# The two heads' values products of a pair, issued chunk by chunk as two column tiles of one PSUM bank

## The chip, the cores and the metric

The kernel runs on one NeuronCore of a Trainium2 chip. Its time is the device time in microseconds of one execution. A core has TensorE (PE, which multiplies matrices and writes PSUM; its weight loads are shown apart as PEld), VectorE (DVE), ScalarE (ACT), GpSimd (POOL), SyncE (SP, which issues most of the DMAs here) and 16 DMA engines. All arithmetic is in float32.

## The reference

Attention with normalised queries and keys, and then a feed-forward block whose activation is a softmax-weighted linear unit. 8 sequences of 448 tokens, 12 heads of 64, so x has 3584 rows of 768; the hidden width is 1024. The weights come as float64.

```python
q_n, k_n = (rmsnorm(q, g_q), rmsnorm(k, g_k))
scores = scale * np.matmul(q_n, k_n.transpose(0, 1, 3, 2))
scores = scores - np.max(scores, axis=-1, keepdims=True)
attn = np.exp(scores)
attn = attn / (np.sum(attn, axis=-1, keepdims=True) + 1e-09)
attn_out = np.matmul(attn, v)                       # the values product
x = attn_out.transpose(0, 2, 1, 3).reshape(B * S, H * D)
h = x @ w_in
e = np.exp(h - h.max(-1)); sm = e / (e.sum(-1) + 1e-09)
solu = h * sm
out = ((solu - mean) / np.sqrt(var + 1e-06) * g_ln) @ w_out
```

## The kernel before, in words

Attention goes by pairs of heads: `n` counts 48 pairs, six to a sequence (`NP = 6`). The 448 tokens of a sequence are taken as four chunks of 112 (`NJ = 4`, `SP = 112`). For a pair, `load` fetches q, k and v; `norm` squares (ACT), sums (DVE), takes the power -1/2 (POOL) and scales q and k (`qkn`, DVE and POOL); `qk_transpose` transposes both heads at once on PE into `pt` and copies them out with the gain (`qkT`, DVE). Since the heads' 64 columns lie side by side, head 0 stands in partitions 0 to 63 of `qkT` and head 1 in 64 to 127.

`scores(n, j)` multiplies chunk j of the queries with all keys. The two heads use different halves of the array's rows (64x128 tiles at rows 0 and 64) and different PSUM banks of one tile `s`. DVE takes the maximum `nmax`, ACT the exponential into `E` with its sum. `normalise` divides on POOL, one instruction per head. `e_transpose(n, h, half)` transposes `E` of a head on PE, two chunks of keys at a time, through `pe`, and ACT and DVE copy it to `ET`. `values(n, h)` multiplies v with `ET`: four matmuls, one per chunk of keys, accumulate 64 rows of `o`. Head 0 writes partitions 0 to 63 of the one PSUM tile `o`, head 1 partitions 64 to 127: 128x64 tiles of the array at columns 0 and 64. After head 1, DVE copies `o` to `xT`, the transposed x.

The feed-forward block takes 128 tokens at a time: `ff_in` (`h`), `ff_solu`, `ff_transpose` (`pu`) and `ff_out` (`po`). Each float32 matmul that is no transpose stands in the profile as two weight loads and two matmul records; a transpose stands as one of each. So the 384 values matmuls are 768 records of `o`, and a head's four matmuls are "x8".

The order in which the program is written comes from `pair`: between the four `scores` of pair n stand the transposes of `E` and the values of pair n - 1, head 0's values after `scores(n, 1)`, head 1's after `scores(n, 3)`, and then `qk_transpose(n + 1)`. The pieces of the feed-forward of the sequence before are spread over pairs 2 to 6 of each sequence; the first pair of a sequence gets none (below: an unfilled pair). In sequence 0 there is no feed-forward; instead the weights are converted from float64, largely on DVE. At the very end stand the last pair's transposes and values and the feed-forward of the last sequence. The framework then schedules each engine's instructions from this order, so that what stands in an engine's queue differs somewhat from what is written; each engine runs its queue as it stands. Tile pools give the buffers: PSUM has two of `s` or `h` and four of tag `t`, which `pt`, `pe`, `pu`, `po` and `o` share; `ET` has two.

Of the kernel before, what the change touches and what calls it, by code (L numbers as in the profile page):

```python
# [9 lines left out]
FP32 = mybir.dt.float32  # L10
# [8 lines left out]
def kernel(  # L19
# [12 lines left out]
    nc = tc.nc  # L32
    B, H, S, D = q.shape
    DM, DFF = moe_w_in.shape
    P = 128
    NJ = 4              # token chunks of one sequence; chunk j holds the tokens NJ * p + j
    SP = S // NJ
    NP = H // 2         # head pairs: two heads fill the 128 partitions of a transposed operand
    KD = DM // P
    KF = DFF // P  # L40
    HO = DM // 2
# [17 lines left out]
    def setup():  # L59
        nc.gpsimd.memset(mhalf, -0.5)  # L60
        make_identity(nc, ident)
        nc.scalar.dma_start(grow[0:KF, :], moe_g_ln.rearrange("(c p) -> c p", p=P))
        for i, g in enumerate((g_q, g_k)):
            for h in range(2):
                nc.scalar.dma_start(grow[KF + i : KF + i + 1, h * D : (h + 1) * D], g.rearrange("(o d) -> o d", o=1))
        pg = ps_t.tile([P, KF + 2], FP32, tag="t", name="pg")
        nc.tensor.transpose(pg, grow, ident[0 : KF + 2, 0 : KF + 2])
        nc.vector.tensor_copy(gcol, pg)
        # the scores' 1 / sqrt(D) goes with the gain of q
        nc.vector.tensor_scalar(gcol[:, KF : KF + 1], gcol[:, KF : KF + 1], float(D) ** -0.5, None, OP.mult)  # L70

    # The weights come as the bits of float64: word 0 of an element holds the low 32 bits of the
    # mantissa, word 1 the sign, 11 bits of exponent and the high 20 bits of the mantissa.
    # value = M * E, M = 1 + high / 2^20 + low / 2^52 rounded to float32 and E = +-2^(exponent - 1023);
    # E is 0 below the range of float32, and infinite above it.

    def w_steps():
        # the parts to convert, in the order in which they are used
        for c in range(KD):
            for half in range(2):  # L80
                yield moe_w_in, w_in, c, slice(half * 512, half * 512 + 512)
        for c in range(KF):
            for half in range(2):
                yield moe_w_out, w_out, c, slice(half * HO, half * HO + HO)
# [11 lines left out]
    def convert_w(step, raw):  # L96
        _, dst, c, cols = step
        n = cols.stop - cols.start
        lo, hi = raw[:, :, 0], raw[:, :, 1]
        tmp = work.tile([P, 2, n], U32, tag="uT", name="tmp")  # L100
        e, m = tmp[:, 0], tmp[:, 1].bitcast(FP32)
        nc.vector.tensor_scalar(tmp[:, 1], hi, 0xFFFFF, None, OP.bitwise_and)
        nc.scalar.activation(m, tmp[:, 1], AF.Copy, scale=2.0 ** -20, bias=1.0)
        nc.vector.scalar_tensor_tensor(m, lo, 2.0 ** -52, m, OP.mult, OP.add)
        nc.vector.tensor_scalar(e, hi, 20, 0x7FF, OP.logical_shift_right, OP.bitwise_and)
        ei = e.bitcast(I32)
        nc.vector.tensor_scalar(ei, ei, 896.0, 0.0, OP.subtract, OP.max)
        nc.vector.tensor_scalar(ei, ei, 255.0, 2.0 ** 23, OP.min, OP.mult)
        nc.vector.scalar_tensor_tensor(e, hi, 0x80000000, e, OP.bitwise_and, OP.bitwise_or)
        if dst is w_in:  # L110
            nc.gpsimd.tensor_tensor(dst[:, c, cols], m, e.bitcast(FP32), OP.mult)
        else:
            # the gain of the layer norm goes into the rows of w_out
            nc.vector.scalar_tensor_tensor(
                dst[:, c, cols], m, gcol[:, c : c + 1], e.bitcast(FP32), OP.mult, OP.mult
            )

    st = {}
    xTs = {}

# [1 line left out]

    def load(n):
        b, hp = divmod(n, NP)
# [74 lines left out]
    def e_transpose(n, h, half):  # L199
        d = st[n]  # L200
        if half == 0:
            d["ET", h] = work.tile([SP, NJ, S], FP32, tag="ET", name="ET")
        for kc in (2 * half, 2 * half + 1):
            pt = ps_t.tile([SP, S], FP32, tag="t", name="pe")
            for j in range(NJ):
                nc.tensor.transpose(  # L206
                    pt[:, j * SP : (j + 1) * SP], d["E"][:, h, j, kc * SP : (kc + 1) * SP], ident[0:SP, 0:SP]
                )
            (nc.vector.tensor_copy if kc % 2 else nc.scalar.copy)(d["ET", h][:, kc], pt)  # L209

    def values(n, h):
        b, hp = divmod(n, NP)
        d = st[n]
        if b // 2 not in xTs:
            xTs[b // 2] = work.tile([P, KD, 2 * S], FP32, tag="xT", name="xT")
        if h == 0:
            d["o"] = ps_t.tile([P, S], FP32, tag="t", name="o")
        for kc in range(NJ):
            nc.tensor.matmul(  # L219
                d["o"][h * D : (h + 1) * D, :], d["v"][:, h, kc * D : (kc + 1) * D], d["ET", h][:, kc],  # L220
                start=(kc == 0), stop=(kc == NJ - 1),
            )
        if h == 1:
            # back to the order of the tokens
            c0 = (b % 2) * S
            nc.vector.tensor_copy(  # L226
                xTs[b // 2][:, hp, c0 : c0 + S].rearrange("d (p j) -> d j p", j=NJ),
                d["o"].rearrange("d (j p) -> d j p", j=NJ),
            )
            del st[n]  # L230

# [1 line left out]

    mt = {}

# [8 lines left out]
            )  # L244

    def ff_solu(m, t):
        # with u = h * exp(h - max) and s = sum + 1e-9: solu = u / s, so that
        # (solu - mean) / sqrt(var + 1e-6) = (u - mean_u) / sqrt(var_u + 1e-6 * s * s)
        d = mt[m, t]
        nmax = small.tile([P, 1], FP32, tag="hmax", name="hmax")  # L250
        nc.vector.tensor_reduce(nmax, d["h"], AX, OP.max, negate=True)  # L251
        u = d["u"] = work.tile([P, DFF], FP32, tag="u", name="u")
        s = small.tile([P, 1], FP32, tag="hsum", name="hsum")
        nc.scalar.activation(u, d["h"], AF.Exp, bias=nmax, accum_out=s)
        nc.vector.tensor_tensor(u, d["h"], u, OP.mult)
        bs = small.tile([P, 2, 6], FP32, tag="bs", name="bs")
        mv = small.tile([P, 2], FP32, tag="mv", name="mv")
        for half in range(2):
            nc.vector.bn_stats(out=bs[:, half], in_=u[:, half * 512 : half * 512 + 512])
        nc.vector.bn_aggr(out=mv, in_=bs)  # L260
        e = small.tile([P, 1], FP32, tag="he", name="he")
        nc.vector.tensor_scalar(s, s, 1e-9, None, OP.add)
        nc.vector.tensor_scalar(e, s, s, 1e-6, OP.mult, OP.mult)
        nc.vector.tensor_tensor(e, e, mv[:, 1:2], OP.add)  # L264
        nc.gpsimd.tensor_tensor(e, e, mhalf, OP.pow)  # L265
        nc.vector.tensor_scalar(u, u, mv[:, 0:1], e, OP.subtract, OP.mult)
# [23 lines left out]
            del mt[m, t]  # L290

    def feed_forward(b):
        # the tiles of 128 tokens that are whole once sequence b is done
        m, n0 = b // 2, S // P
        tiles = range(0, n0) if b % 2 == 0 else range(n0, 2 * S // P)

        def first(t):
            return [lambda: ff_in(m, t, 0), lambda: (ff_in(m, t, 1), ff_solu(m, t))]

        def second(t):  # L300
            return [lambda: ff_transpose(m, t), lambda: ff_out(m, t, 0), lambda: ff_out(m, t, 1)]

        prev = None
        for t in tiles:
            yield from first(t)
            if prev is not None:
                yield from second(prev)
            prev = t
        yield from second(prev)

    def pair(n):
        # scores of pair n; the values of the pair before it come between them
        pieces = []
        for j in range(NJ):
            pieces.append(lambda j=j: scores(n, j))
            if n:
                h, half = divmod(j, 2)
                pieces.append(lambda h=h, half=half: e_transpose(n - 1, h, half))
                if half:
                    pieces.append(lambda h=h: values(n - 1, h))  # L320
            if j == 1 and n + 3 < B * NP:
                pieces.append(lambda: load(n + 3))
            if j == 1 and n + 1 < B * NP:
# [13 lines left out]
    raw = load_w(wsteps[0])  # L337
    for b in range(B):
        fill = list(feed_forward(b - 1)) if b else []
        # the last pair of a sequence gets its values within the next sequence's first pair  # L340
        flat = [p for i in range(NP) for p in pair(b * NP + i)]
        lead = len(pair(b * NP))
        done = 0
# [13 lines left out]
    for h in range(2):  # L357
        for half in range(2):
            e_transpose(B * NP - 1, h, half)
        values(B * NP - 1, h)  # L360
    for p in feed_forward(B - 1):
        p()

# [29 lines left out]
```

## Time and profile before

| | us |
|---|---|
| time, median of 3 runs | 1561.86 (1561.26 to 1563.79) |
| span of the profiled execution, first to last instruction | 1558.0 |
| the part of the median outside that span | 3.9 |
| PE busy | 1401.2 (90%) |
| DVE, POOL, ACT busy | 783.5, 536.8, 484.3 |
| the scores of sequences 0, 1 and 2 begin in the trace at | 14.9, 191.8, 377.3 |
| the last values product ends at | 1466.9 |

The page has no time of its own for the profiled execution beside the span; the span and the 3.9 us together are taken as its time. The trace thus has three stages: sequence 0 with the conversion of the weights (0 to 192), sequences 1 to 7 with feed-forward work between (192 to 1463), and the last feed-forward alone (to 1558). In rows of instructions "x" is a count; "mean ns" is the length of one record, which for matmuls overlaps with its neighbours, so that the distance from start to start is what an instruction takes of PE. In brackets stands the idle time of the engine before the row and what ended it.

### The profile page before, as it was taken

The numbers are of one execution on the slowest core, as the hardware profiler recorded it, in microseconds if no ns is written. First come the engines' busy times: TensorE is split into PE (matmuls) and PEld (weight loads), VectorE is DVE, ScalarE is ACT, GpSimd is POOL, SyncE is SP. The second block draws the span as 40 slices with busy tenths as digits, with TensorE's granted clock in tenths as the row PEclk, the third lists the DMA queues.
The fourth block names the chain that finished last, engine by engine and source line by source line (L and its number), as shares of the span: only waits on it lengthen the run. The fifth ranks groups of instructions, "written<-read, shape, count | busy, mean of one in ns | idle before, by whom it ended". The sixth has DMA issues, their size and how long they took to land.

```text
span 1558.0 us, 14064 instructions
## 1 busy us (share of the span) xinstructions
PE 1401.2 (90%) x5249; PEld 658.7 (42%) x5249; DVE 783.5 (50%) x1234; ACT 484.3 (31%) x1177; POOL 536.8 (34%) x239
## 2 busy tenths in 40 slices
PE   4676578999899998999899998899899998999998
PEld 2232233444344443444344453344444454444454
DVE  7988874444445444543354434635453344534231
ACT  4333342324223332332333234234322233323111
POOL 5543373333432324334323243343423243231100
PEclk8677779999999999999999999999999999999999
DMA  4322210011010011001000110010100001000000
GB/s 136 111 86 79 85 42 18 28 36 38 19 42 31 18 38 36 18 28 46 29 18 28 33 51 18 24 40 29 46 18 28 29 28 34 6 16 11 11 11 31
DMA packets 42716, 57.53 MB, mean 37 GB/s; under 512 B 3216, under 2 KB 35480, under 8 KB 42648
## 3 DMA queue, kind: packets, MB, share of 16 engines
q1 hardware_dynamic: 38592, 45.62, 9.7%
q10 hardware_dynamic: 4056, 11.02, 1.8%
q8 instruction: 41, 0.67, 0.2%
q14 instruction: 27, 0.22, 0.0%
HBM read 45.62 MB, written 11.01 MB: 36 GB/s over the span
## 4 chain that ended last, share of the span: by engine, by line
PE 65%; DVE 18%; POOL 6%; ACT 5%; DMA 4%; issue 2%; SPq 0%; ACTq 0%; POOLq 0%; DVEq 0%
PE o L219 18%; PE po L285 17%; PE h L242 14%; PE s L180 7%; PE pe L206 7%; POOL E L195 4%; DMA qk<-in_k_dram 3%; DVE nmax L184 3%; PE pt L165 2%; ACT E L186 2%; DVE xT L226 2%; DVE rs L138 2%; DVE qkT L170 2%; POOL rs L144 1%; DVE qkn L152 1%
## 5 line engine op out<-in xcount | busy, mean ns | idle before, releaser
L195 POOL TENSOR_TENSOR E<-E,sum 112x1792 f32<-112x1792 f32 x96 | 305.5, 3201 | 274.0 <-DVE sum L193 261.0
L219 PE MATMUL o<-ET,v 112*64 112x448 f32 x768 | 351.0, 579 | 23.7 <-DVE ET L209 20.4
L242 PE MATMUL h<-w_in,xT 128*128 128x512 f32 x672 | 307.7, 605 | 5.4 <-ACT E L186 5.4
L285 PE MATMUL po<-w_out,uT 128*128 128x384 f32 x896 | 302.2, 490 | 2.1 <-DVE ET L209 1.1
L186 ACT ACTIVATE E<-s,nmax 112x448 f32<-112x448 f32 x384 | 240.2, 632 | 198.0 <-DVE nmax L184 194.8
L184 DVE TENSOR_REDUCE nmax<-s 112x2 f32<-112x896 f32 x192 | 207.1, 1082 | 153.3 <-PE s L180 153.3
L180 PE MATMUL s<-qkT 64*112 64x448 f32 x768 | 214.0, 620 | 47.7 <-DVE qkT L170 36.8
L206 PE MATMUL pe<-ident,E 112*112 112x112 f32 x1536 | 193.2, 273 | 51.2 <-POOL E L195 46.8
L206 PEld LDWEIGHTS pe<-ident,E 112*112 112x112 f32 x1536 | 155.9, 138 | 165.6 <-issue 81.8
L144 POOL TENSOR_TENSOR rs<-rs,mhalf 112x16 f32<-112x16 f32 x48 | 141.9, 2958 | 233.5 <-DVE rs L143 223.8
L285 PEld LDWEIGHTS po<-w_out,uT 128*128 128x128 f32 x896 | 166.0, 190 | 125.3 <-issue 13.8
L242 PEld LDWEIGHTS h<-w_in,xT 128*128 128x128 f32 x672 | 123.8, 192 | 160.5 <-issue 153.2
L219 PEld LDWEIGHTS o<-ET,v 112*64 112x64 f32 x768 | 91.7, 141 | 193.7 <-issue 106.0
L209 ACT COPY ET<-pe 112x448 f32<-112x448 f32 x192 | 101.1, 531 | 192.5 <-PE pe L206 191.4
L209 DVE COPY ET<-pe 112x448 f32<-112x448 f32 x192 | 117.8, 616 | 71.8 <-PE pe L206 70.7
L265 POOL TENSOR_TENSOR he<-he,mhalf 128x1 f32<-128x1 f32 x28 | 15.3, 548 | 319.3 <-DVE he L264 319.3
L180 PEld LDWEIGHTS s<-qkT 64*112 64x112 f32 x768 | 59.6, 182 | 146.2 <-issue 59.0
L251 DVE TENSOR_REDUCE hmax<-h 128x1 f32<-128x1024 f32 x28 | 34.3, 1225 | 168.9 <-PE h L242 168.6
L286 ACT COPY y<-po 128x384 f32<-128x384 f32 x56 | 26.7, 477 | 262.6 <-PE po L285 262.6
L136 ACT ACTIVATE sq<-qk 112x1024 f32<-112x1024 f32 x48 | 50.9, 1060 | 181.5 <-DMA qk<-in_k_dram 150.3
L138 DVE TENSOR_REDUCE rs<-sq 112x16 f32<-112x1024 f32 x48 | 58.4, 1216 | 96.5 <-ACT sq L136 96.5
L152 POOL TENSOR_TENSOR qkn<-qk,rs 112x512 f32<-112x512 f32 x48 | 56.6, 1179 | 137.5 <-PE pt L165 99.9
(43 smaller groups left out, 756.3 us busy)
## 6 DMA issues: line engine op xcount, KB each, us to landing
qk<-in_q_dram SPq DMA_DIRECT2D x48, 224.0 KB, 2.8
qk<-in_k_dram SPq DMA_DIRECT2D x48, 224.0 KB, 3.1
v<-in_v_dram SPq DMA_DIRECT2D x48, 224.0 KB, 2.6
out_dram<-y ACTq DMA_DIRECT2D x28, 384.0 KB, 2.3
raw<-in_moe_w_in_dram SPq DMA_DIRECT2D x12, 512.0 KB, 3.5
raw<-in_moe_w_out_dram SPq DMA_DIRECT2D x16, 384.0 KB, 3.0
grow<-in_g_q_dram ACTq DMA_DIRECT2D x2, 0.2 KB
grow<-in_g_k_dram ACTq DMA_DIRECT2D x2, 0.2 KB
```

What stands on the lines that cost most here:

```text
L138: nc.vector.tensor_reduce(rs.rearrange("p s h j -> p (s h j)"), sq.rearrange("p s h (j d) -> p (s h j) d", d=D), AX, OP.add,)
L144: nc.gpsimd.tensor_tensor(rs.rearrange("p s h j -> p (s h j)"), rs.rearrange("p s h j -> p (s h j)"), mhalf[0:SP].to_broadcast([SP, 4 * NJ ...
L152: eng.tensor_tensor(d["qkn"][:, s].rearrange("p j h d -> p h j d"), d["qk"][:, s].rearrange("p h (j d) -> p h j d", d=D), rs[:, s].rearran ...
L180: nc.tensor.matmul(s[:, h, 0:S], d["qkT"][hh, 0, j * SP : (j + 1) * SP], d["qkT"][hh, 1, :], start=True, stop=True)
L184: nc.vector.tensor_reduce(nmax, s[:, :, 0:S], AX, OP.max, negate=True)
L186: nc.scalar.activation(d["E"][:, h, j], s[:, h, 0:S], AF.Exp, bias=nmax[:, h : h + 1], accum_out=d["sum"][:, h, j : j + 1])
L195: nc.gpsimd.tensor_tensor(d["E"][:, h], d["E"][:, h], d["sum"][:, h].rearrange("p j -> p j ()").to_broadcast([SP, NJ, S]), OP.mult)
L206: nc.tensor.transpose(pt[:, j * SP : (j + 1) * SP], d["E"][:, h, j, kc * SP : (kc + 1) * SP], ident[0:SP, 0:SP])
L209: (nc.vector.tensor_copy if kc % 2 else nc.scalar.copy)(d["ET", h][:, kc], pt)
L219: nc.tensor.matmul(d["o"][h * D : (h + 1) * D, :], d["v"][:, h, kc * D : (kc + 1) * D], d["ET", h][:, kc], start=(kc == 0), stop=(kc == NJ ...
L242: nc.tensor.matmul(d["h"][:, hs], xTs[m][:, c, t * P : (t + 1) * P], w_in[:, c, hs], start=(c == 0), stop=(c == KD - 1))
L285: nc.tensor.matmul(po, d["uT"][:, c], w_out[:, c, hs], start=(c == 0), stop=(c == KF - 1))
```

## The change

`values` no longer takes a head. Called once per pair, at the place of head 1's values before, it goes through the four chunks of keys and issues for each chunk head 0's matmul and then head 1's. The `o` tile lives from there to its copy instead of from head 0's values on. `ET` has three buffers instead of two.

```diff
@@ e_transpose
-            d["ET", h] = work.tile([SP, NJ, S], FP32, tag="ET", name="ET")
+            d["ET", h] = work.tile([SP, NJ, S], FP32, tag="ET", name="ET", bufs=3)
@@ values
-    def values(n, h):
+    def values(n):
...
-        if h == 0:
-            d["o"] = ps_t.tile([P, S], FP32, tag="t", name="o")
+        o = ps_t.tile([P, S], FP32, tag="t", name="o")
         for kc in range(NJ):
-            nc.tensor.matmul(
-                d["o"][h * D : (h + 1) * D, :], d["v"][:, h, kc * D : (kc + 1) * D], d["ET", h][:, kc],
-                start=(kc == 0), stop=(kc == NJ - 1),
-            )
-        if h == 1:
...
+            for h in range(2):
+                nc.tensor.matmul(
+                    o[h * D : (h + 1) * D, :], d["v"][:, h, kc * D : (kc + 1) * D], d["ET", h][:, kc],
+                    start=(kc == 0), stop=(kc == NJ - 1),
+                )
...
@@ pair
-                if half:
-                    pieces.append(lambda h=h: values(n - 1, h))
+                if j == NJ - 1:
+                    pieces.append(lambda: values(n - 1))
@@ the last pair
     for h in range(2):
         for half in range(2):
             e_transpose(B * NP - 1, h, half)
-        values(B * NP - 1, h)
+    values(B * NP - 1)
```

The queue of PE in an unfilled pair (the first of sequence 5), before. Counts here are matmuls of the program, of which `s`, `o`, `h` and `po` have two records each in the profile:

```order
L180 MATMUL s<-qkT 112x448 x2
L206 MATMUL pe<-ident,E 112x112 x8
L180 MATMUL s<-qkT 112x448 x2
L206 MATMUL pe<-ident,E 112x112 x8
L219 MATMUL o<-ET,v 64x448 x4
L180 MATMUL s<-qkT 112x448 x2
L206 MATMUL pe<-ident,E 112x112 x8
L180 MATMUL s<-qkT 112x448 x2
L206 MATMUL pe<-ident,E 112x112 x8
L219 MATMUL o<-ET,v 64x448 x2
L165 MATMUL pt<-ident,qkn 128x112 x2
L219 MATMUL o<-ET,v 64x448
```

Such a pair after the change (the values stand on line 221 now):

```order
L180 MATMUL s<-qkT 112x448 x2
L206 MATMUL pe<-ident,E 112x112 x8
L180 MATMUL s<-qkT 112x448 x2
L206 MATMUL pe<-ident,E 112x112 x8
L180 MATMUL s<-qkT 112x448 x2
L206 MATMUL pe<-ident,E 112x112 x8
L180 MATMUL s<-qkT 112x448 x2
L206 MATMUL pe<-ident,E 112x112 x8
L221 MATMUL o<-ET,v 64x448 x8
L165 MATMUL pt<-ident,qkn 128x112 x8
L206 MATMUL pe<-ident,E 112x112 x12
```

Head 0's four matmuls have moved down past two scores and two transposes, and head 1's, which were split by transposes of q and k, stand together with them.

In the program of before no two neighbouring values matmuls belong to different heads. In the changed one, counted over PE's whole queue, 318 neighbours do. Taken two by two from the front of each run, they make 180 couples of one matmul of each head, out of 192 that are possible; after the fifth pair of heads 165 out of 172. In the first five pairs of heads, transposes of q and k and scores stand between, and three couples are left of four; here the first values of the program, on PE:

```order
L221 MATMUL o<-ET,v 64x448
L180 MATMUL s<-qkT 112x448 x2
L221 MATMUL o<-ET,v 64x448 x2
L165 MATMUL pt<-ident,qkn 128x112 x4
L221 MATMUL o<-ET,v 64x448 x4
L165 MATMUL pt<-ident,qkn 128x112 x4
L221 MATMUL o<-ET,v 64x448
```

The values matmuls stand in 183 runs before and in 66 after. Places in PE's queue at which the shape of the tile changes (128x128, 64x128 for scores, 128x64 for values) are 674 before and 477 after; past the fifth pair's values, 599 and 412.

On DVE the end of the unfilled pair reads so before:

```order
L170 TENSOR_SCALAR qkT<-pt,gcol 128x448
L226 COPY xT<-o 128x4x112
L170 TENSOR_SCALAR qkT<-pt,gcol 128x448
L192 TENSOR_SCALAR sum<-sum 112x8
L152 TENSOR_TENSOR qkn<-qk,rs 112x2x4x64
```

and so after:

```order
L192 TENSOR_SCALAR sum<-sum 112x8
L193 RECIPROCAL sum<-sum 112x8
L227 COPY xT<-o 128x4x112
L170 TENSOR_SCALAR qkT<-pt,gcol 128x448 x2
L209 COPY ET<-pe 112x448
L152 TENSOR_TENSOR qkn<-qk,rs 112x2x4x64
```

The copy of `o` now stands ahead of both copies of `qkT`, and the sums and their reciprocal, on which POOL's division waits, ahead of all three.

More of the change, by code (lines that the diff above doesn't have):

```diff
@@ L215, in values @@
             xTs[b // 2] = work.tile([P, KD, 2 * S], FP32, tag="xT", name="xT")
-        if h == 0:
-            d["o"] = ps_t.tile([P, S], FP32, tag="t", name="o")
+        o = ps_t.tile([P, S], FP32, tag="t", name="o")
         for kc in range(NJ):
-            nc.tensor.matmul(
-                d["o"][h * D : (h + 1) * D, :], d["v"][:, h, kc * D : (kc + 1) * D], d["ET", h][:, kc],
-                start=(kc == 0), stop=(kc == NJ - 1),
-            )
-        if h == 1:
[L225 to L230, printed above, removed]
+            for h in range(2):
[3 more added lines that the diff above has]
+                )
+        c0 = (b % 2) * S
+        nc.vector.tensor_copy(
+            xTs[b // 2][:, hp, c0 : c0 + S].rearrange("d (p j) -> d j p", j=NJ),
+            o.rearrange("d (j p) -> d j p", j=NJ),
+        )
+        del st[n]
     mt = {}
```

## The prediction

> **What bounds the kernel now.** I read the page first: busy times, the slices of the span, and the chain that ended last.
>
> ```profile
> span 1558.0 us, 14064 instructions
> PE 1401.2 (90%) x5249; PEld 658.7 (42%) x5249; DVE 783.5 (50%) x1234; ACT 484.3 (31%) x1177; POOL 536.8 (34%) x239
> PE   4676578999899998999899998899899998999998
> ...
> DVE  7988874444445444543354434635453344534231
> PE 65%; DVE 18%; POOL 6%; ACT 5%; DMA 4%; issue 2%; SPq 0%; ACTq 0%; POOLq 0%; DVEq 0%
> ```
>
> PE is at nine tenths from the fifth of the slices on; DVE is the fuller engine only at the start, and the chain has 65% in PE. The stages, in time windows (busy us of PE, PEld, DVE, ACT, POOL; then the granted clock), and of the first one what the records of `o` alone take:
>
> ```profile
> 0.00:192.00 192.00, 117.42 (x395) 50.10 (x397) 163.52 (x272) 65.33 (x152) 86.46 (x43) 0.75 0.33 101
> 192.00:1463.00 1271.00, 1194.10 (x4594) 562.23 (x4595) 596.45 (x922) 408.00 (x1005) 448.14 (x192) 0.98 0.09 29
> 1463.00:1558.00 95.00, 89.71 (x264) 46.36 (x261) 23.56 (x42) 10.99 (x20) 2.16 (x4) 1.00 0.04 17
> 0.00:192.00 192.00, 46.50 (x80) 10.72 (x80) 4.73 (x5) 0.75 0.33 101
> 377.00:1292.00 915.00, 861.23 (x3316) 407.70 (x3316) 423.23 (x660) 292.89 (x721) 317.96 (x138) 0.99 0.10 31
> ```
>
> So 192 us are mostly DVE's (163.5 busy), 1271 are PE's (94% busy, DVE under half), and 95 are feed-forward alone, which the change does not touch. In five full sequences (last row, 30 pairs of heads) PE is idle for 915 - 861.2 = 53.8 us, 1.8 us per pair. What one PE instruction costs I take from groups by shape (busy us, mean ns) and from the timeline:
>
> ```profile
> L219 PE MATMUL o<-ET,v 112*64 112x448 f32 x768 | 351.0, 579 | 23.7 <-DVE ET L209 20.4 <-ACT ET L209 3.1
> L180 PE MATMUL s<-qkT 64*112 64x448 f32 x768 | 214.0, 620 | 47.7 <-DVE qkT L170 36.8 <-ACT E L186 8.5 <-DVE hsum L262 2.3
> 823.34 3.22 PE L219 MATMUL o<-ET,v 112*64 112x448 f32 x8
> 824.52 0.14 PEld L219 LDWEIGHTS o<-ET,v 112*64 112x64 f32 x1 [0.24 <-issue]
> 824.89 0.14 PEld L219 LDWEIGHTS o<-ET,v 112*64 112x64 f32 x1 [0.24 <-issue]
> 824.52 0.54 PE L219 MATMUL o<-ET,v 112*64 112x448 f32 x1
> 814.46 0.63 PE L180 MATMUL s<-qkT 64*112 64x448 f32 x2
> 814.46 1.01 PE L180 MATMUL s<-qkT 64*112 64x448 f32 x4
> ```
>
> Of `o`, one head's eight records take 3.22 us. The last is 0.54 long, so seven steps take 2.68, 0.383 each; the weight loads step by 0.37 to 0.38. I take 0.376 us of PE per record: they follow each other, none overlaps more than its tail. The scores show the contrast. Same number of records, same 448 columns, but 214.0 us busy against 351.0: two records, one of each head, are both under way within 0.63 us, the length of one, and all four end after 1.01 = one step of 0.38 and one length. Matmuls on two parts of the array do run at once here, in float32, and though each comes as two records.
>
> **The change, part by part.** *Column tiles side by side.* Before, head 0's and head 1's values never stand next to each other; after, 165 couples do past the fifth pair of heads. If a couple runs at once, as the scores' couples do, each saves one matmul, two records: 165 x 2 x 0.376 = 124.1 us of PE. The scores show it for two parts of the rows; here both heads use the same 112 partitions and differ in columns, so PE must read two streams from the same partitions. Nothing in the trace shows two moving streams so. The nearest row is a weight load under a running matmul, which reads the same partitions twice at once: the load at 824.52 begins with the matmul of 824.52, and its successor still follows 0.37 later. Ends: 0 saved (no overlap) and 124.1; I take 124.1, because the scores' row is the nearest.
>
> The Trainium skill, "TensorE: Matmul & The Clock Gate", Part 3 (row/col tiling), has a measured gain of 2.38 for three column tiles, which is 1.26 slots for three; if two needed 1.26 slots as well, an estimate by that page would keep 0.74 of the gain, 92 us instead of 124, and the sum would end 32 us higher.
>
> *Changes of the tile's shape.* The price is in a pair of windows where values follow the feed-forward, beside a run of the latter:
>
> ```profile
> 822.92 0.49 PE L285 MATMUL po<-w_out,uT 128*128 128x384 f32 x1
> 823.34 0.59 PE L219 MATMUL o<-ET,v 112*64 112x448 f32 x1
> 818.07 5.34 PE L285 MATMUL po<-w_out,uT 128*128 128x384 f32 x16
> ```
>
> Sixteen `po` records take 5.34 with a last one of 0.49, so 0.323 from start to start; from the last `po` to the first `o` it is 0.42, 0.09 to 0.10 more. I take 0.093. Past the fifth pair the queue has 599 - 412 = 187 fewer such changes: 17.4 us. Ends: 0, where PE waits there for something else anyway, and 18.
>
> *Sequence 0.* DVE sets most of it, and the clock is 0.75. Its 80 records of `o` occupy 46.5 us; half of that, 23, is the most that could go, nothing the least. What waited there:
>
> ```profile
> DVE qkn L152 <- POOL rs L144: 11.9, 6, 3.0
> ...
> DVE xT L226 <- PE o L219: 5.5, 4, 2.6
> ```
>
> DVE waited for the values for 5.5 us only. I take 4.
>
> *What becomes late next.* In the other 43 pairs PE loses about 3.3 us of work each (141.5 / 43), and its waits can grow, since other engines' work was covered by it. The unfilled pair shows the covers:
>
> ```profile
> 930.80:947.60 16.80, 15.29 (x73) 6.69 (x72) 9.76 (x15) 8.60 (x22) 3.93 (x2) 1.00 0.08 28
> 980.70:1015.40 34.70, 29.91 (x111) 13.21 (x110) 19.38 (x27) 9.90 (x24) 12.99 (x7) 0.90 0.11 34
> 946.13 0.94 DVE L226 COPY xT<-o 128x448 f32<-128x448 f32 x1 [0.59 <-PE o L219]
> 947.48 0.16 DVE L192 TENSOR_SCALAR sum<-sum 112x8 f32<-112x8 f32 x1
> 947.62 0.63 PE L180 MATMUL s<-qkT 64*112 64x448 f32 x2 [1.53 <-DVE qkT L170]
> 948.52 6.30 POOL L195 TENSOR_TENSOR E<-E,sum 112x1792 f32<-112x1792 f32 x2 [2.20 <-DVE sum L193]
> 951.75 1.75 PE L206 MATMUL pe<-ident,E 112*112 112x112 f32 x16 [2.36 <-POOL E L195]
> ```
>
> DVE and ACT have 9.8 and 8.6 us of work in it, so at 16.8 - 3.3 = 13.5 us they still fit; the fuller pair has 19.4 us of DVE in 34.7. No engine becomes the bound by its amount of work. The waits at its end are 1.53 (the copies of `qkT`, behind the copy of `o` on DVE) and 2.36 (POOL's division, which began only once DVE, behind those copies, had done the sums). In the new DVE queue the sums stand ahead of these copies, so POOL starts while the eight values matmuls run. `qkT` comes as late as before: copy of `o` and two `qkT` copies after the last values. I take 1 us off for each of the 7 unfilled pairs (between 2.4 off and 1 more). In the 36 filled pairs I add 0.4 us each, a little over a fifth of the 1.8 they wait on average; the ends are 0 (the feed-forward covers) and 3.3 (everything saved is waited). The nearest row for it is the list of what PE waits for past 192 us, which is short and spread:
>
> ```profile
> PE pe L206 <- POOL E L195: 24.2, 14, 3.1
> PE s L180 <- DVE qkT L170: 15.4, 8, 4.7
> PE o L219 <- DVE ET L209: 13.2, 7, 3.1
> ...
> PE pu L275 <- ACT ET L209: 5.9, 7, 1.5
> ```
>
> The third `ET` buffer lets the next pair's first head be transposed while both old `ET` are still read; it costs no instruction. That `o` holds a shared PSUM buffer for a few us instead of half a pair can only ease waits like the last row's; I count nothing. The loads of q, k and v move little on SP, and their covers stay: nothing above waits for a DMA in the middle stage.
>
> *Sum.* 1558.0 - 124.1 - 17.4 - 4 - 7 + 14 = 1419.5 us; with the 3.9 us by which the median of the runs is above the span, 1423.
>
> **The rivals.** *No overlap.* Column tiles may run one after the other, and the change then does not do what it says. For it: no row shows two streams from the same partitions. Against: the scores. Only the 17.4 us of shape changes are left: 1562 - 17 = 1545, still faster.
>
> *Slower.* Without overlap, alternating columns could also expose the weight load at each step from one head to the other: 318 steps x 0.14 us (the length of a load in the row at 824.52) = 45 us, less the 17.4: 1562 + 27 = 1589. It decides once a step costs more than 17.4 / 318 = 55 ns. For it: in no row does a load into other columns run under a matmul. Against: loads into the very same columns do, at 824.89 in the middle of a run.
>
> The Trainium skill, same page and part, says that a weight load overlaps a running matmul only when the row group differs, and here both heads use the same rows; by that rule this rival would come. The trace already disagrees for the single head: loads and matmuls of `o` share all rows, and the step is 0.38 and not 0.38 + 0.14.
>
> *Waits take half back.* The overlap comes, but filled pairs wait for `ET`, `E` and `qkT` half of what they saved: 36 x 1.65 = 59 instead of 14, so 1468. For it: `values` now needs both heads' last copies, with the copies made just ahead. Against: the same wait stood before head 1, and DVE is busy 423 of 915 us.
>
> *One step more per pair.* If matmuls start strictly in order, a couple's second record and the next head's first overlap only staggered: nine steps in place of eight, 43 x 0.376 = 16 us, 1439. This is within the forecast.
>
> **How the numbers follow.** Overlap with waits about as now: 0.72 (own range 1380 to 1460: from 23 instead of 4 us saved in sequence 0, 17 off in unfilled pairs and 0 added in filled ones, to the staggered start with some 20 us of waits more). Waits take half or more: 0.13, up to 1500. No overlap: 0.08. Slower: 0.05; 0.02 for what I did not think of. The range for 8 in 10 takes the first two, less the far ends of the first, which would need all three terms at their best at once: 1390 to 1500. About 0.2% (3 us) is what a measurement of this kernel can tell from no change. Faster by more: 0.72 + 0.13 + 0.07 = 0.92; within: 0.02; slower: 0.06.
>
> **What would show it.** Right: `o` busy near 190 us instead of 351 with a mean still near 540 to 580 ns; a run of sixteen `o` records of about 3.2 us, two under way at a time; the first sequence still near 190 us; an unfilled pair of 13 to 14 us. The shape changes: `pt` following `o` seldom. Wrong: sixteen records in 6.2 us (no overlap), weight loads of `o` with PE idle beside them (slower), or PE's waits for `ET` and `E` of over 100 us in the middle stage (half taken back).

## The result, and the profile after

The changed kernel takes 1441.9 us (median of 4 runs, 1438.2 to 1448.0) against 1562.1 before: a ratio of 0.923, 95% interval 0.921 to 0.926. The forecast was 1423 with a range of 1390 to 1500. The profiled execution took 1442.7 us, its span 1440.9.

Of the page after, the same lines as before, and then two rows of its timeline:

```profile
span 1440.9 us, 14104 instructions
PE 1246.6 (87%) x5249; PEld 630.5 (44%) x5249; DVE 803.3 (56%) x1234; ACT 482.0 (33%) x1177; POOL 548.6 (38%) x239
PE   3466558899899998899899998899899998999998
...
PE 44%; DVE 23%; POOL 12%; DMA 8%; issue 6%; ACT 6%; SPq 1%; ACTq 0%; POOLq 0%; DVEq 0%
L221 PE MATMUL o<-ET,v 112*64 112x448 f32 x768 | 173.1, 558 | 16.2 <-DVE ET L209 15.8
875.77 3.23 PE L221 MATMUL o<-ET,v 112*64 112x448 f32 x16
876.20 0.92 PE L221 MATMUL o<-ET,v 112*64 112x448 f32 x4
```

The same number of values records is busy for 173.1 us in place of 351.0, and each is as long as before (558 ns on average against 579). The last two rows are of one pair of heads: sixteen records in 3.23 us, as long as one head's eight took; in a window 0.1 us wide, four records are in progress, two couples that are 0.38 us apart. PE's share of the chain falls from 65% to 44%, DVE's, POOL's and DMA's rise.

The three stages in time windows (busy PE, PEld, DVE, ACT, POOL; clock):

```profile
0.00:190.30 190.30, 100.64 (x393) 46.10 (x394) 164.16 (x271) 65.36 (x152) 89.91 (x43) 0.72 0.34 102
190.30:1348.90 1158.60, 1059.27 (x4601) 538.68 (x4601) 615.79 (x923) 405.64 (x1005) 456.47 (x192) 0.97 0.10 32
1348.90:1440.90 92.00, 86.70 (x256) 45.75 (x256) 23.38 (x41) 11.00 (x20) 2.17 (x4) 1.00 0.05 18
```

Sequence 0 lasts 190.3 us in place of 191.8 while PE is busy 17 us less in it: it is DVE's, with 164 us busy as before. All but 1.5 us of the gain lies in the seven sequences that follow. (The last window begins here where the values products end; the one of the kernel before began 4 us ahead of that point, so 95 and 92 us are not to be compared.)

To split those into work and waits I took, for each two matmul records that follow each other, the distance of their starts less the step of the first one's kind (0.376 us for `o` and `s`, 0.429 for `h`, 0.3225 for `po`, 0.0957 for `pe` and `pt`, 0.109 for `pu`, 0.093 more where the tile's shape changes; a partner that starts within 0.07 us counts as it is). From the first score of sequence 1 to the end, work falls from 1209.9 to 1068.9 us, by 141.0, and waits rise from 151.4 to 176.8, by 25.4. 141.0 - 25.4 + 1.5 is the 117.1 us by which the span is shorter.

Not all that this split calls a wait is idle time of PE. From the first score of sequence 1 to the end (before, then after, in windows):

```profile
191.80:1558.00 1366.20, 1283.96 (x4856) 608.75 (x4856) 620.21 (x963) 418.99 (x1025) 450.30 (x196) 0.98 0.09 28
190.30:1440.90 1250.60, 1145.97 (x4856) 584.44 (x4856) 639.17 (x964) 416.64 (x1025) 458.64 (x196) 0.97 0.10 31
```

PE is idle for 82.2 us before and 104.6 after, 22.4 more. The rest of the waits, 69 us before and 72 after, are steps that took longer than their kind's while PE was busy; the granted clock was 0.98 before and 0.97 after. So the growth is idle time but for some 3 us.

What PE waits for past sequence 0, after (waited for, us, times, longest), in place of the list that the prediction quotes:

```profile
PE s L180 <- ACT E L186: 27.7, 17, 2.9
PE h L243 <- ACT E L186: 19.6, 13, 2.7
PE pe L206 <- POOL E L195: 12.7, 9, 2.8
PE s L180 <- DVE qkT L170: 11.8, 5, 4.0
```

The first two are new in that size: in the trace before, `s` waited 6.2 us for ACT's exponential there and `h` 5.4. Scores and `h` share two PSUM buffers, and such a buffer comes free when the exponentials have read it. An unfilled pair of 13 to 14 us, one of the signs of being right, did not come: those of sequences 2 to 7 take 15.8 to 19.0. The waits for POOL's division and for `qkT` became shorter (24.2 and 15.4 before).

### The profile page after: what moved, and what is told of

Read it like the earlier page. It is cut to its first block, busy times and chain, and to the rows that moved or that the text cites. A ratio compares the mean times of both kernels' runs of the same rounds, so it can differ in the third digit from the quotient of the medians.

```text
span 1440.9 us, 14104 instructions
## 1 busy us (share of the span) xinstructions
PE 1246.6 (87%) x5249; PEld 630.5 (44%) x5249; DVE 803.3 (56%) x1234; ACT 482.0 (33%) x1177; POOL 548.6 (38%) x239
## 4 chain that ended last, share of the span: by engine, by line
PE 44%; DVE 23%; POOL 12%; DMA 8%; issue 6%; ACT 6%; SPq 1%; ACTq 0%; POOLq 0%; DVEq 0%
PE po L286 15%; PE h L243 14%; POOL E L195 8%; DMA qk<-in_k_dram 7%; PE o L221 6%; PE s L180 5%; DVE nmax L184 5%; PE pe L206 4%; ACT E L186 3%; DVE rs L138 2%; DVE qkn L152 2%; POOL rs L144 2%; DVE qkT L170 2%; POOL qkn L152 2%; ACT sq L136 2%
## 5 line engine op out<-in xcount | busy, mean ns | idle before, releaser
L195 POOL TENSOR_TENSOR E<-E,sum 112x1792 f32<-112x1792 f32 x96 | 309.7, 3247 | 234.6 <-DVE sum L193 233.3
L243 PE MATMUL h<-w_in,xT 128*128 128x512 f32 x672 | 317.3, 622 | 19.6 <-ACT E L186 19.6
L286 PE MATMUL po<-w_out,uT 128*128 128x384 f32 x896 | 306.8, 495 | 14.0 <-ACT ET L209 8.6
L184 DVE TENSOR_REDUCE nmax<-s 112x2 f32<-112x896 f32 x192 | 207.5, 1083 | 140.4 <-PE s L180 140.2
L206 PE MATMUL pe<-ident,E 112*112 112x112 f32 x1536 | 200.8, 277 | 43.2 <-POOL E L195 40.8
L206 PEld LDWEIGHTS pe<-ident,E 112*112 112x112 f32 x1536 | 161.0, 141 | 163.8 <-issue 88.6
L243 PEld LDWEIGHTS h<-w_in,xT 128*128 128x128 f32 x672 | 128.1, 198 | 177.3 <-issue 154.3
L221 PE MATMUL o<-ET,v 112*64 112x448 f32 x768 | 173.1, 558 | 16.2 <-DVE ET L209 15.8
L266 POOL TENSOR_TENSOR he<-he,mhalf 128x1 f32<-128x1 f32 x28 | 15.4, 550 | 299.8 <-DVE he L265 299.8
L227 DVE COPY xT<-o 128x448 f32<-128x448 f32 x48 | 46.5, 968 | 98.5 <-PE o L221 98.2
L221 PEld LDWEIGHTS o<-ET,v 112*64 112x64 f32 x768 | 53.6, 138 | 98.6 <-issue 73.2
```

Source lines behind the costliest of these rows:

```text
L184: nc.vector.tensor_reduce(nmax, s[:, :, 0:S], AX, OP.max, negate=True)
L195: nc.gpsimd.tensor_tensor(d["E"][:, h], d["E"][:, h], d["sum"][:, h].rearrange("p j -> p j ()").to_broadcast([SP, NJ, S]), OP.mult)
L206: nc.tensor.transpose(pt[:, j * SP : (j + 1) * SP], d["E"][:, h, j, kc * SP : (kc + 1) * SP], ident[0:SP, 0:SP])
L221: nc.tensor.matmul(o[h * D : (h + 1) * D, :], d["v"][:, h, kc * D : (kc + 1) * D], d["ET", h][:, kc], start=(kc == 0), stop=(kc == NJ - 1),)
L243: nc.tensor.matmul(d["h"][:, hs], xTs[m][:, c, t * P : (t + 1) * P], w_in[:, c, hs], start=(c == 0), stop=(c == KD - 1))
L286: nc.tensor.matmul(po, d["uT"][:, c], w_out[:, c, hs], start=(c == 0), stop=(c == KF - 1))
```

## The experiments

**Is it overlap, and does it need the heads side by side?** Three kernels keep the change's place, buffers and pieces, and alter only how the two heads stand within a values product.

Head 0 first, then head 1:

```diff
-        for kc in range(NJ):
-            for h in range(2):
+        for h in range(2):
+            for kc in range(NJ):
```

> The changed kernel, but within the values product head 0's four matmuls are issued first and then head 1's four; place, tile, buffers and everything else stay. Theory A (the gain is overlap, and it needs matmuls of different columns next to each other in the queue): only the one joint per pair of heads can overlap, so nearly all of the 124 us comes back; 1441 + 7/8 x 135 = about 1555 us, a run of sixteen records of o takes about 5.8 us. Theory B (PE starts any queued matmul whose columns are free, however the heads are ordered within the run): about 1441 us, a run of 3.2 us. Theory C (the gain is the regrouping, fewer changes of the tile's shape and the later place, not overlap): also about 1441 us, but with runs of o near 6 us.

In blocks of two chunks, so that the heads stand 0 0 1 1 0 0 1 1:

```diff
-        for kc in range(NJ):
-            for h in range(2):
+        for k2, h, i in [(k2, h, i) for k2 in range(2) for h in range(2) for i in range(2)]:
+            kc = 2 * k2 + i
+            if True:
```

> The changed kernel, with the heads alternating in blocks of two chunks (two matmuls of head 0, two of head 1, and again). Theory A with starts strictly in the queue's order: a run of sixteen records needs 13 steps of 0.376 us in place of 8, so 48 x 5 x 0.376 = 90 us come back, about 1531 us. Theory A with a look-ahead of two matmuls, or Theory B: 8 steps, about 1441 us. Theory C: about 1441 us.

Alternating as in the change, but both heads on the same columns:

```diff
-                    o[h * D : (h + 1) * D, :], d["v"]...
-                    start=(kc == 0), stop=(kc == NJ - 1),
+                    o[0:D, :], d["v"]...
+                    start=(kc == 0 and h == 0), stop=(kc == NJ - 1 and h == 1),
...
+        nc.scalar.copy(xTs[b // 2][D:P, ...], o[0:D]...)
```

> The changed kernel with both heads' matmuls on the same columns: order and place as in the change, but head 1 writes partitions 0 to 63 too, accumulated onto head 0 (so the two heads' values are summed, which the reference does not ask), and the sum is copied to both halves of xT, the upper half by ACT. The queue stays as in the change and nothing can overlap. Theories A and B: 180 couples x 2 records x 0.376 = 135 us come back, 1576 us, a run of o near 6.2 us. Theory C: 1441 us, up to 1450 for the second copy.

Measured: 1482.5 us for head after head, 1445.7 in twos, 1534.8 on the same columns, against 1441.9 for the change. A run of sixteen records in each (in this order):

```profile
561.37 4.78 PE L221 MATMUL o<-ET,v 112*64 112x448 f32 x16
549.56 3.28 PE L222 MATMUL o<-ET,v 112*64 112x448 f32 x16
518.01 6.23 PE L221 MATMUL o<-ET,v 112*64 112x448 f32 x16
```

The same column gives 6.23 us, sixteen steps of 0.376 and a tail (the 0.2 us by which the last record is longer than its step): with nearly the same queue nothing overlaps, and the time is 93 us over the change, not the 135 expected. (The same columns are also the same rows of PSUM; these runs do not part the two.) So the gain is overlap of columns, and Theory C falls; without the overlap 1534.8 is left, still 27 to 29 us under the kernel before (its ratio is 0.982, 0.979 to 0.984). Neither A nor B fits head after head: 4.78 us are twelve steps, not sixteen and not eight. Its windows near the start, in the middle and near the end show where the overlap lies:

```profile
561.80 0.91 PE L221 MATMUL o<-ET,v 112*64 112x448 f32 x2
562.92 0.97 PE L221 MATMUL o<-ET,v 112*64 112x448 f32 x4
565.24 0.92 PE L221 MATMUL o<-ET,v 112*64 112x448 f32 x2
```

Two records in progress are one stream and its predecessor's tail; four are two streams. The couples stand in the middle alone, from the fifth step to the eighth: head 1's first four records start beside head 0's last four, ahead of records that stand before them in the queue. That gave a new theory: a record may start beside the oldest waiting one if at most three records stand between them. It fits 0 0 1 1 too, where exactly three do.

**The look-ahead, tried with another order.** 0 0 0 1 1 1 0 1:

```diff
-        for kc in range(NJ):
-            for h in range(2):
+        for h, kc in [(0, 0), (0, 1), (0, 2), (1, 0), (1, 1), (1, 2), (0, 3), (1, 3)]:
+            if True:
```

> The changed kernel with the order 0 0 0 1 1 1 0 1 of the heads in a values product. Theory from the two earlier orders (PE can start a record beside the oldest unfinished one if at most three other unstarted records stand between them): steps are r1, r2, r3 with r7, r4 with r8, r5 with r9, r6 with r10, r11 with r13, r12 with r14, r15, r16: ten steps, a run of 10 x 0.376 + 0.2 = 3.97 us, about 20 us over the change: 1460 us. Rival (only whole blocks of two matmuls pair up): twelve steps or more, a run of 4.7 us or more, 1480 us. Rival (any order overlaps fully within eight matmuls unless one head comes first entirely): 3.2 us, 1442 us.

```profile
552.31 4.03 PE L221 MATMUL o<-ET,v 112*64 112x448 f32 x16
```

4.03 us are ten steps and the tail, as the new theory had it; its couples start after two single steps, and the last two records are single. The time is 1451.7 us, 10 over the change and not 20. The split shows where the rest of the longer runs went: past sequence 0, work is 66 us more than in the change for head after head, 120 on the same columns and 41 here, but waits are 21, 28 and 33 us less. The trace does not name the head of a record; what belongs to which is read from the count of steps.

**The third ET buffer.**

```diff
-            d["ET", h] = work.tile([SP, NJ, S], FP32, tag="ET", name="ET", bufs=3)
+            d["ET", h] = work.tile([SP, NJ, S], FP32, tag="ET", name="ET")
```

> The changed kernel with two ET buffers in place of three; the order of matmuls on PE stays. Theory: the third buffer matters little, since a pair's values end before the next pair's first copies into ET are due: 1436 to 1450 us. Rival: the first transposes of the next pair then wait for the values of the old one, about 1 us per pair: 1490 us.

1441.5 us (1437.4 to 1445.1): it brings and costs nothing that shows.

**Why the waits grew.** Two kernels test the score buffers from two sides. The first gives scores and `h` a third buffer at the expense of the others:

```diff
-    ps_s = ctx.enter_context(tc.tile_pool(name="ps_s", bufs=2, ...
-    ps_t = ctx.enter_context(tc.tile_pool(name="ps_t", bufs=4, ...
+    ps_s = ctx.enter_context(tc.tile_pool(name="ps_s", bufs=3, ...
+    ps_t = ctx.enter_context(tc.tile_pool(name="ps_t", bufs=2, ...
```

> The changed kernel with three PSUM buffers for scores and h, and two in place of four for the tag t, since PSUM has no more. Theory (PE waits for scores' buffers): its waits for ACT's exponential, 34.2 + 19.6 us in the change, fall under 20; the tag t then runs short, its waits for copies into ET grow from 12 to some 60 us, and the order has 532 shape changes in place of 477; net 1440 to 1500 us. Rival (those waits are of ACT's work and not of the buffers): the waits for the exponential stay over 40 us.

1511.0 us. PE's waits in it, the largest ones, and the one for the exponential:

```profile
PE pe L206 <- ACT ET L209: 33.1, 23, 4.6
PE pt L165 <- DVE xT L227: 28.2, 31, 3.6
PE pe L206 <- DVE ET L209: 20.6, 23, 1.9
...
PE s L180 <- ACT E L186: 6.0, 4, 1.9
```

With a third buffer the scores wait 6.0 us for the exponential over the whole span, in place of 34.2, and `h` is not among the waits at all. That speaks for the buffers, though the new waits for copies also give the exponentials more time. The unfilled pairs of sequences 2 to 7 take 14.5 to 14.9 us in place of 15.8 to 19.0. With two buffers for everything else the kernel as a whole is slower than the change, a little over the end of the range expected. PE's idle time past sequence 0 is the same (105.5 us, 104.6 in the change): the waits have moved. The profiled run is longer by 8.5 us in sequence 0, by 22 us of work in the split, and by steps longer than their kind's, at a granted clock of 0.95 where the change had 0.97.

The second shortens what a buffer waits for: the maximum is left out.

```diff
-        nmax = small.tile([SP, 2], FP32, tag="nmax", name="nmax")
-        nc.vector.tensor_reduce(nmax, s[:, :, 0:S], AX, OP.max, negate=True)
...
-                d["E"][:, h, j], s[:, h, 0:S], AF.Exp, bias=nmax[:, h : h + 1], accum_out=...
+                d["E"][:, h, j], s[:, h, 0:S], AF.Exp, accum_out=...
```

> The changed kernel without the maximum: the exponential is taken of the scores as they are, so the reduction on DVE (1.08 us for each pair of score chunks) is left out and ACT can start when the scores are written. Theory: the new waits of PE are for score buffers in PSUM, which come free with the exponential (34.2 and 19.6 us in the trace of the change, 8.5 and 5.4 before); without the reduction most of the growth goes, 40 us less: about 1400 us. Rival: PE is held by POOL's division and the copies of qkT, which this leaves alone: 1432 to 1442 us.

1343.1 us, 99 under the change, where 40 were expected. Part of the miss is sequence 0, which DVE sets: 160.8 us in place of 190.3. The rest is waits: past sequence 0 they fall from 176.8 to 107.4 us by the split above, 51 us of it idle time. The list of them, and an unfilled pair (windows; the change's, then this kernel's):

```profile
PE po L284 <- ACT ET L207: 13.5, 3, 4.7
PE pe L204 <- POOL E L193: 7.9, 9, 3.3
...
PE s L180 <- ACT E L184: 5.0, 9, 1.8
866.80:882.60 15.80, 12.92 (x87) 7.14 (x86) 10.34 (x16) 9.10 (x23) 7.43 (x3) 1.00 0.13 40
799.10:812.20 13.10, 12.83 (x87) 7.12 (x86) 6.43 (x12) 7.99 (x23) 7.43 (x3) 1.00 0.14 48
```

Of the 47.3 us of waits for the exponential (`s` and `h`) 5.0 are left, and the unfilled pair takes 13.1 us, PE's own work in it. That is about what I had forecast for it with the maximum in place (16.8 - 3.3 = 13.5, and 1 less).

**Is that what ate the gain?** If so, the change must bring all of it where there is no maximum. The kernel before without the maximum, to stand against the changed one without it:

> The kernel before, without the maximum (as in e6_no_max, which is the changed kernel without it: 1343.1 us). With both, the change's gain is had where scores' buffers come free early. Theory (the part of the 141.5 us that the change did not bring was eaten by PE's waits for the chain of maximum and exponential): without the maximum the change brings all of it and what sequence 0 gives, 141 to 158 us, so this kernel takes 1484 to 1501 us. Rival (it was eaten by POOL's division, the copies of qkT and the copies into ET): the change brings about 120 us here as well, so 1463 us.

1510.6 us, so the change brings 167 us here, where it brings 120 with the maximum. By the traces: sequence 0 takes 188.1 and 160.8 us, a gain of 27 that the theory did not foresee in this size (with DVE relieved, PE may count there too; that was not tested); past it, waits are 108.5 us in this kernel and 107.4 in the changed one, by the split into work and waits above. With the maximum they grew by 25.4, without it not at all. Idle time alone grew by 22.4 us with it and by 4.5 without (48.8 and 53.3; this kernel, then the changed one):

```profile
188.10:1506.10 1318.00, 1269.21 (x4856) 616.99 (x4856) 446.20 (x786) 377.37 (x1022) 437.43 (x190) 0.98 0.09 29
160.80:1340.50 1179.70, 1126.44 (x4856) 580.79 (x4856) 494.39 (x805) 376.94 (x1025) 455.20 (x194) 0.98 0.11 33
```

So the maximum is what the growth hangs on. Leaving it out frees the score buffers earlier and also takes 207.5 us of work off DVE; these two are not parted here.

**A cover for the unfilled pairs.** Instead of shortening the wait, put work under it: three feed-forward pieces are kept for the next sequence's first pair.

```diff
+    carried = []
     for b in range(B):
-        fill = list(feed_forward(b - 1)) if b else []
+        fill = carried + (list(feed_forward(b - 1)) if b else [])
+        nc_ = len(carried)
+        keep = 3 if 0 < b < B - 1 else 0
+        carried, fill = fill[len(fill) - keep :], fill[: len(fill) - keep]
...
-            due = len(fill) * max(0, x + 1 - lead) // (len(flat) - lead)
+            due = nc_ + (len(fill) - nc_) * max(0, x + 1 - lead) // (len(flat) - lead)
+            if x + 1 < lead:
+                due = nc_ * (x + 1) // lead
```

> The changed kernel, but the last three pieces of a sequence's feed-forward (a transposition and two output products, about 11 us of PE) are kept for the next sequence's first pair, which had none, in sequences 2 to 7. Theory: the first pairs lose the gain because no feed-forward covers their waits (3.7 to 4.6 us each in the trace of the change); with cover about 3.5 us each come back, 6 x 3.5 = 21 us: 1421 us. Rival: the waits belong to a chain through DVE, ACT and POOL that sets the pace of pairs wherever the feed-forward stands, and only move to the pairs that lose their pieces: 1436 to 1446 us.

1433.1 us, a ratio of 0.918 (0.915 to 0.920) to before: 9 us better than the change, between theory and rival and nearer to the rival. Its longest waits that the change did not have so:

```profile
PE s L180 <- ACT E L186: 17.6, 22, 2.4
PE pe L206 <- ACT y L287: 15.6, 7, 2.7
```

The scores' waits for the exponential halve, but transposes now wait for PSUM buffers that ACT's copy of the output products has still to empty; that wait was 0.6 us in the change.

The later feed-forward and the missing maximum in one kernel:

> The change, e5_carry's later feed-forward and e6_no_max's missing maximum together. If the two gains are of different waits: 1343 - 9 = 1334 us. If the first pairs of sequences have nothing left to cover once the maximum is gone (13.1 us each, about the 12 us of PE's own work in them): 1343 us.

Both edits together take 1333.1 us, a ratio of 0.854 (0.852 to 0.856) and the fastest here: the two gains add. Leaving out the maximum changes the result only through the 1e-9 in the sum, but it gives up the guard against an overflow of the exponential, so with the maximum kept the best version is the one at 1433.1 us.

## Why the prediction was right, and where it was off

- *Column tiles side by side, 124.1 us, and changes of shape, 17.4 us.* Right: 141.0 us of work went, past sequence 0, of the 141.5 counted. I had taken the end given by the scores' row, and two streams from the same partitions run at full step. The sign named for the shapes, `pt` seldom right behind `o`, came only in part: 51 times in the trace, 80 before.
- *The rival "no overlap", 1545.* The kernel on one column shows that case: 1534.8, 27 under the kernel before where I had 17. By the split, work past sequence 0 is 21 us less, waits 2 and sequence 0 another 2.
- *The rival "slower".* It did not come: alternating costs no step in any run here. By the Trainium skill, "TensorE: Matmul & The Clock Gate", Part 3, a load overlaps a running matmul only where the row group differs; the trace disagrees, with both heads on the same rows and a run of 3.23 us, whose steps of 0.376 us hide loads of 0.14. The same section of the Trainium skill has matmuls start strictly in order; head after head disagrees with that as well, with twelve steps in place of fifteen. An estimate from the gain of 2.38 that the Trainium skill gives there for three tiles would have left 0.74 of the overlap's gain for two; here a couple takes one step.
- *One step more per pair.* It did not come either: 3.23 us are eight steps and the tail, so the start of a couple's second record does not hold up the next head's first.
- *Sequence 0, 4 us.* 1.5 us. DVE, busy 164 us in it, sets its length as I had said; its wait for the values fell from 5.5 us to 4.2.
- *What becomes late next, +7 us.* This is the step that was off; measured, +25.4. By the same split of the trace, the filled pairs wait 133.2 us in place of 117.0, 16.2 more, where I had 14. The unfilled pairs of sequences 1 to 7 wait 41.5 in place of 32.9, 8.6 more, where I had 7 less. So most of the miss lies in the unfilled pairs; about 3 us of their 8.6 are those of sequence 7, whose pair took 19.0 us at a granted clock of 0.91 where the others took 15.8 to 16.5. That the filled pairs came near 14 is in part luck: 0.4 us a pair was a share chosen without a row for it, and their waits were not followed one by one. I had priced only the two waits that the row of the old trace showed at the pair's end, and those did shrink as said: the sums now stand ahead on DVE, and PE waits 1.38 us for POOL there instead of 2.36. What I missed, in the unfilled pairs, is a wait that the old trace does not show because head 0's values covered it. In the changed kernel it stands in the middle of the pair (timeline):

```profile
868.37 1.22 DVE L138 TENSOR_REDUCE rs<-sq 112x16 f32<-112x1024 f32 x1 [4.86 <-ACT sq L136]
868.66 1.01 PE L180 MATMUL s<-qkT 64*112 64x448 f32 x4
869.50 1.08 DVE L184 TENSOR_REDUCE nmax<-s 112x2 f32<-112x896 f32 x1
870.68 0.63 ACT L186 ACTIVATE E<-s,nmax 112x448 f32<-112x448 f32 x1 [1.11 <-DVE nmax L184]
871.31 0.62 ACT L186 ACTIVATE E<-s,nmax 112x448 f32<-112x448 f32 x1
872.08 1.01 PE L180 MATMUL s<-qkT 64*112 64x448 f32 x4 [1.50 <-ACT E L186]
```

The third scores need the first ones' buffer. That is read by the maximum, which stands behind the sum of squares on DVE, and then by two exponentials; it comes free at 871.9. Before, head 0's values stood on PE just there (the same pair in the old trace):

```profile
934.49 3.40 PE L219 MATMUL o<-ET,v 112*64 112x448 f32 x8
937.82 1.01 PE L180 MATMUL s<-qkT 64*112 64x448 f32 x4
```

They took 3.3 us, and the third scores followed without a wait. I asked what else PE's lost work had covered, but looked for it where the values now stand, not at the place that head 0's had left.

- *The sum.* The span is 21.4 us over the forecast one: 18.4 from the waits, 2.5 from sequence 0, 0.5 from the work.

## What to carry to other kernels

Where two accumulations have at most 64 output rows each, put them on different columns of one bank and issue them close together; not strictly alternating, since blocks of two were as good here, but not one whole accumulation after the other. When PE work is moved, look at both ends: what the new place delays, and what the old place has covered; a resource with few buffers that was refilled behind it becomes the next wait. A pass over the scores that only frees a buffer later (here the maximum, ahead of the exponential) can hold up PE although its engine is far from full; how much of that is the buffer and how much the load on DVE, these runs do not tell.

## What the runs showed of the hardware that was not expected

PE starts float32 matmul records out of the queue's order when they are on other columns: 8, 10, 12 and 16 steps for sixteen records in the orders 01010101 or 00110011, 00011101, 00001111, and all on one column. All four fit a look-ahead of three records past the oldest waiting one, which is read from the counts of steps, since the trace does not name a record's head; whether PE itself or what feeds it does this, the traces do not tell.
